# Longformer attention with a snake MLP on one core: where the lying keys and queries, w_out and the global columns are handled

## The chip, the cores and the metric

The kernel runs on one core of one Trainium2 chip. The metric is the device time of one execution in microseconds (us). The engines are named as in the profile: PE is the matrix engine (PEld its weight loads), DVE the vector engine, ACT the scalar engine with the activation functions, POOL the GpSimd engine, SP the engine that does nothing but issue DMAs. Each engine takes its instructions in the order in which the program emits them, so an instruction that waits holds up all that is emitted behind it on the same engine. POOL issues the DMAs that convert float32 to bfloat16 ("software" queue), SP those that do not ("hardware" queue).

## The reference

Inputs are q, k, v of 8 images (batch B) x 8 heads (H) x 576 tokens (S) x 64, eight global token indices, and the weights of a two layer MLP (512 to 2048 to 512). Attention is banded with a half width of 32, with rows and columns of the global tokens open:

```python
mask = np.abs(pos[:, None] - pos[None, :]) <= window          # window = 32
mask = mask | is_global[:, None] | is_global[None, :]
attn = softmax(where(mask, scale * q @ k.T, -1e9)); attn_out = attn @ v
h = x @ w_in                    # x: attn_out as 4608 rows of 512
s = np.sin(alpha * h)
g = h + s * s / (alpha + 1e-09)
out = g @ w_out
```

## The kernel before

**Stages.** The kernel treats one image (b = 0 to 7) at a time. `attention(b)` computes scores, exponentials, products with the values and denominators for four head pairs (hp) and leaves the normalised result, features on partitions, in `xTs[b]` (4 chunks of 128 features x 576 tokens). `gemm1(b)` multiplies with w_in in 16 groups (nt) of 128 features: eight matmuls of 288 columns a group, then on ACT the sine (`sb`), on ACT or DVE its square (`s2`; `ON_ACT...` lists the groups whose square is ACT's), on DVE the sum that is written into `H2[:, nt, ...]`. The result banks rotate over three PSUM tiles: group 0 zn, 1 zr, 2 zd, 3 zn and so on, so group nt + 3 has to wait for DVE's `H2` of group nt. Even images lie in columns 0 to 575 of H2, odd ones in 576 to 1151, and the 64 rows of the global tokens of all images in the last 64 columns.

**gemm2 as filler.** The second product, `gemm2(b)`, is a generator. It covers the 1152 columns of an image pair in blocks of 128: four blocks for even b, five for odd b, each block sixteen matmuls of 128x512, then an ACT copy `osb` and a store. `fill(n)` takes n matmuls from it wherever the program has put a `fill`: in `attention` 1 (START), then `FIRST` and `SECOND` around the two halves of the scores of each head pair, then `NEAR` and `MIDST`; in `gemm1` `PER_GROUP[nt]` after the matmuls of each group (`GROUP_LAST` for the last image). What is left at the end is done after the last `gemm1`, ahead of `gemm2_globals()` (the 64 global rows, result in zd) and of `gemm2(7)`.

**Global tokens.** Their rows of q, k, v of all images are gathered into `gq`, `gk`, `gv`, which lie in rows of H2 that are not yet in use (nt 13, 14, 15). `turn_kq()` turns them in bank `zo[1]` at the start of group 4 of `gemm1(0)`; `cast_globals_v()` on POOL converts gv. At the very end the normalised global rows (`global_rows`, lines 1064 to 1071) are put into the last columns of `xTs[7]`, and `put_globals()` (POOL, eight copies of 128x16) moves the columns of image 7's global tokens over the ordinary ones in H2. Where they go is computed in `load_columns()`: seven tiny DVE instructions, then eight register loads on POOL, behind head pair 3 of attention(5).

**Image 1's keys and queries.** They are loaded "lying" (48 rows of 48 x 64 values for each of k, q and each head parity t; `load_lying`, four DMAs of 288 KB on POOL) into the second halves of the tiles KD and VD. Attention(0) still uses these, so `load_lying(0)` is emitted behind the last head pair and `load_lying(1)` behind the last products. Then follow on POOL `cast_v(1)`, `load_w_out()` (four DMAs), and on SP `load_v(1)`. In `gemm1(0)` PE turns them in three thirds (`turn_lying`, 64 transposes each, at nt = 7, 9, 11) into the banks `zo[0]` (queries) and `zo[1]` (keys); `place_lying` copies each third to `KX[1]` (one DVE copy, at nt = 8, 10, 12) and to `QX[1]` (two ACT copies, at nt = 9, 11, 13). A third can be turned only when the copies of the one before have read the banks.

Of the kernel before, what the change touches and what calls it, by code (L numbers as in the profile page):

```python
# [10 lines left out]
ALU = mybir.AluOpType  # L11
AF = mybir.ActivationFunctionType
DT = mybir.dt
# [236 lines left out]
def kernel(  # L250
# [183 lines left out]
    def load_w_out():  # L434
# [11 lines left out]
    HK = HH * NT12  # L446
    nat = {w: H2[0 : D + HK, 2 + 3 * w : 5 + 3 * w, :].rearrange("p n c -> p (n c)")[:, 0 : KT * D] for w in (0, 1)}
    gq, gk, gv = [
        H2[0 : NG * B, nt, 0 : 2 * H * D].bitcast(DT.float32).rearrange("p (h d) -> p h d", d=D)
        for nt in (13, 14, 15)  # L450
    ]

    banks = mctx.enter_context(tc.tile_pool(name="banks", bufs=1, space=PSUM))
    zn, zd = [banks.tile([P, 2, 512], DT.float32, name=name) for name in ("zn", "zd")]
# [127 lines left out]
    load_v0((1, 2))  # L582
    load_w_in((1,))
    load_v0((3,))
    load_w_in((2, 3))
    load_vg0()
    gather(q, gq)

# [115 lines left out]
    for e, c0 in ((0, 20), (1, 16)):  # L704
        own = M2[:, :, e].rearrange("p t (x c) -> p t x c", x=2)[:, :, :, c0 : c0 + 24]
        nc.vector.tensor_tensor(out=own, in0=own, in1=farv[:, :, e], op=ALU.max)

    lie = [t[:, NHP * NT12 * D :] for t in (kflat, vflat)]

    def load_lying(t):  # L710

        for w, src in ((1, k), (0, q)):
            nc.gpsimd.dma_start(
                out=lie[t][D * w : D * w + NHP * NT12],
                in_=src[1].rearrange("(hp t) (i r) d -> t hp i (r d)", t=2, r=KT)[t],
            )

    R16 = KT // 3
    lain = [z.bitcast(DT.bfloat16)[:, 0 : R16 * NHP * NT12] for z in (zo[0][:], zo[1][:])]
# [219 lines left out]
    def attention(b, beside):  # L939
# [117 lines left out]
        inverse(last)  # L1057
        nc.scalar.preload_act_table(AF.Sin)
        fill(MIDST)
        numerators(last)  # L1060
        beside(NHP)
        after.release()

    def global_rows(bs):

        nc.vector.reciprocal(out=GR[:, :, :, bs], in_=GD[:, :, :, bs])
        if bs.stop == B:
            nc.vector.tensor_tensor(
                out=xTs[B - 1][:, :, S:SG], in0=GN[:].rearrange("p h j b -> p h (j b)"),
                in1=GR[:].rearrange("p h j b -> p h (j b)"), op=ALU.mult,  # L1070
            )


    spare = [kflat, vflat]
# [62 lines left out]


    ON_ACT = (1, 3, 5, 7, 9, 11, 13)
    ON_ACT_FIRST = (1, 3, 5, 7, 8, 10, 12, 14)  # L1140
    ON_ACT_SECOND = (1, 3, 5, 7, 9, 10, 12, 13)

    def gemm1(b):


        while len(waiting) > 1:
            fill(1)
        xT = xTs[b]
        r0 = (b % 2) * S
        more = b == B - 1  # L1150
        W = SG if more else S
        hr = tc.alloc_tile_pool(name="hr", bufs=1, space=PSUM)
        hs = {}

        def chunks(nt, cs, parts=slice(0, 2)):
            if nt not in hs:
                hs[nt] = (zn, None, zd)[nt % 3] or hr.tile([P, 2, 512], DT.float32, name="zr")
            h = hs[nt]
            for c in cs:
                for h_part, lo, hi in halves(h, W)[parts]:  # L1160
                    nc.tensor.matmul(  # L1161
                        out=h_part, lhsT=w_in[:, c, nt * P : (nt + 1) * P], rhs=xT[:, c, lo:hi],
                        start=(c == 0), stop=(c == CT - 1), skip_group_check=True,
                    )

        on_act = (ON_ACT_FIRST, ON_ACT_SECOND, ON_ACT)[min(b, 2)]
        for nt in range(NT):
            if b == 1 and nt in (10, 12):
                for which, t, y in PLACES[nt - 6 : nt - 4]:
                    place(2, which, t, y, nc.vector.tensor_copy)  # L1170
            if b == 0 and 8 <= nt < 14:
                third, late = divmod(nt - 8, 2)
                place_lying(1 - late, third, nc.scalar.copy if late else nc.vector.tensor_copy)
            if b == 0 and nt == 4:
                turn_kq()
            if b == 0 and nt == 10:

                cast_globals_v()
                for part in range(3):
                    place_globals(1, part, nc.gpsimd.tensor_copy)  # L1180
                load_vg(1)
            if nt == 0:

                for n in range(2):
                    chunks(n, range(CT - 1), slice(0, 2 - more))
                for n in range(2 * more):
                    chunks(n, range(CT - 1), slice(1, 2))
            chunks(nt, range(CT - 1, CT) if nt < 2 else range(CT))
            h = columns(hs[nt], W)
            fill((GROUP_LAST if more else PER_GROUP)[nt])  # L1190
            if b == 0 and nt in (7, 9, 11):
                turn_lying((nt - 7) // 2)
            sb = spool.tile([P, SG], DT.bfloat16, name="sb")
            nc.scalar.activation(out=sb[:, 0:W], in_=h, func=AF.Sin, scale=alphaT[:, nt : nt + 1])  # L1194
            s2 = spool.tile([P, SG], DT.bfloat16, name="s2")
            if nt in on_act:
                nc.scalar.activation(out=s2[:, 0:W], in_=sb[:, 0:W], func=AF.Square)  # L1197
            else:
                nc.vector.tensor_tensor(out=s2[:, 0:W], in0=sb[:, 0:W], in1=sb[:, 0:W], op=ALU.mult)  # L1199
            nc.vector.scalar_tensor_tensor(  # L1200
                out=H2[:, nt, r0 : r0 + W], in0=s2[:, 0:W], scalar=recipT[:, nt : nt + 1], in1=h,
                op0=ALU.mult, op1=ALU.add,
            )
        hr.release()


    columns_of = []

    def load_columns():

        ci = normp.tile([1, 4, NG], DT.int32, name="ci")
        cf = normp.tile([1, 4, NG], DT.float32, name="cf")
        nc.vector.tensor_copy(out=ci[:, 0], in_=gi32[:, 0::2])
# [11 lines left out]
        nc.vector.tensor_scalar(out=gcol[:], in0=cf[:, 3], scalar1=float(S), scalar2=None, op0=ALU.add)  # L1225
        for j in range(NG):
            columns_of.append(nc.gpsimd.value_load(gcol[0:1, j : j + 1], min_val=S, max_val=2 * S - 1))

    def put_globals():


        for j, c in enumerate(columns_of):
            g = 2 * S + j * B + B - 1
            nc.gpsimd.tensor_copy(out=H2[:, :, bass.ds(c, 1)], in_=H2[:, :, g : g + 1])  # L1234

    def gemm2(b):
        lo, hi = (0, 4) if b % 2 == 0 else (4, 9)
        for blk in range(lo, hi):
            ops = zo[(blk + b // 2) % 2]
            osb = osbp.tile([P, DM], DT.float32, name="osb")  # L1240
            parts = 2 if (b, blk) == (B - 1, hi - 1) else 1
            for part in range(parts):
                cols = slice(part * DM // parts, (part + 1) * DM // parts)
                if part:
                    ops = zd[:, 1]
                for nt in range(NT):
                    nc.tensor.matmul(  # L1247
                        out=ops[:, cols], lhsT=H2[:, nt, blk * P : (blk + 1) * P], rhs=w_out[:, nt, cols],
                        start=(nt == 0), stop=(nt == NT - 1), skip_group_check=True,
                    )  # L1250
                    yield True
                nc.scalar.copy(out=osb[:, cols], in_=ops[:, cols])  # L1252
                store(b, blk, osb, cols)

    def store(b, blk, osb, cols):
        c = blk * P
# [26 lines left out]
        )  # L1283


    waiting = []

    def fill(n):
        while n and waiting:
# [3 lines left out]
                n -= 1  # L1293

    START = 1
    FIRST, SECOND = (10, 6, 4, 4), (4, 4, 4, 4)

    NEAR, MIDST = 3, 6
    PER_GROUP = (0, 0, 5) + 11 * (1,) + (0, 0)
    GROUP_LAST = (0, 0, 3) + 13 * (1,)  # L1300

    def places_at(b_att, at):
# [43 lines left out]
    for b in range(B):  # L1346
# [27 lines left out]
    for c in (2, 3):  # L1374
        square_w(c)
        fill(NT)
    judge()
    fill(2 * NT * NT)
    mctx.close()
# [36 lines left out]
```

## Time and profile before

| | us |
|---|---|
| median of 3 runs | 358.66 (358.3 to 359.12) |
| the profiled execution, its own time | 358.42 |
| its span, first to last instruction | 356.7 |
| attention(0) and all loading ahead of it | 0 to 32.7 |
| gemm1(0) | 32.7 to 58.8 |
| attention(1), gemm1(1) | 58.8 to 76.3, 76.3 to 97.0 |
| attention(2), gemm1(2) | 97.0 to 114.0, 114.0 to 134.2 |
| attention(7), gemm1(7) | 284.2 to 301.5, 301.5 to 323.4 |
| rest of gemm2(6), global rows, gemm2(7), checks | 323.4 to 352.2 |
| last store, end of program | 352.2 to 356.7 |

Images 3 to 6 take the same 37 us each as image 2. The profile describes one execution; its times are counted from the start of the span, and 1.7 us of the execution lie outside it. A row of the timeline gives start, duration, engine, source line, operation, output and inputs with the number of instructions merged into it, and in brackets how long the engine was idle just before and what ended the wait. "issue" is a wait for nothing that the profile shows. Matmuls are pipelined: a single 128x512 matmul is shown with some 380 ns, while a row of them advances faster.

### The profile page before, as it was taken

How to read it: one execution, taken by the hardware profiler on the slowest of the kernel's cores; microseconds unless marked ns; L12 is line 12 of the kernel's file. 1: busy time of each engine (PE TensorE's matmuls, PEld its weight loads, DVE VectorE, ACT ScalarE, POOL GpSimd, SP SyncE). 2: the span in 40 equal slices, each digit the busy share in tenths (PEclk: the TensorE clock that was granted, in tenths of full speed). 3: DMA queues.
4: the chain of work that ended last, by engine and by line, in shares of the span. 5: the costliest groups of instructions: out<-in, count | busy, mean ns of one | idle time of the engine just before them, and what ended most of it. 6: DMA issues, size and time to landing. Idle time of an engine off the chain costs nothing.

```text
span 356.7 us, 10900 instructions
## 1 busy us (share of the span) xinstructions
PE 317.8 (89%) x4427; PEld 206.8 (58%) x4484; DVE 274.0 (77%) x536; ACT 286.3 (80%) x428; POOL 58.8 (16%) x85
## 2 busy tenths in 40 slices
PE   1579768999899999999999999899999998999994
PEld 1467555567555764576556655566566645565543
DVE  6785867788979787978798789878887877689630
ACT  6789768997888888988998889688988887878511
POOL 7965420050004000400040004000000000003300
PEclk9999999999999999999999999999999999999998
DMA  7999999669988926694859843993242011001232
GB/s 113 111 139 154 158 217 243 159 110 209 189 161 159 168 65 157 132 190 95 133 87 200 155 107 74 204 162 78 63 96 60 2 57 39 31 0 35 71 92 64
DMA packets 87762, 42.25 MB, mean 118 GB/s; under 512 B 72378, under 2 KB 82362, under 8 KB 87322
## 3 DMA queue, kind: packets, MB, share of 16 engines
q0 software_dynamic: 44944, 18.52, 43.6%
q1 hardware_dynamic: 42762, 22.98, 28.7%
q8 instruction: 36, 0.59, 0.7%
q14 instruction: 20, 0.16, 0.2%
HBM read 41.97 MB, written 20.77 MB: 176 GB/s over the span
## 4 chain that ended last, share of the span: by engine, by line
PE 54%; ACT 16%; DVE 13%; DMA 8%; issue 6%; POOL 0%; DVEq 0%; ACTq 0%; POOLq 0%
PE zo L1247 24%; PE zn L1161 8%; DVE H L1200 6%; PE zr L1161 5%; PE zd L1161 5%; ACT sb L1194 5%; PE ring L971 4%; DMA VD<-in_q_dram 3%; PE zd L1009 2%; DVE s L1199 2%; ACT L947 2%; ACT E L980 2%; PE zn L1009 2%; DMA VD<-vd 2%; ACT s L1197 2%
## 5 line engine op out<-in xcount | busy, mean ns | idle before, releaser
L1247 PE MATMUL zo<-w_out,H 128*128 128x512 bf16 (+1 forms) x519 | 135.2, 376 | 5.7 <-issue 4.8
L1161 PEld LDWEIGHTS <-w_in 128*128 128x128 bf16 x1024 | 99.1, 98 | 47.7 <-issue 15.3
L1247 PEld LDWEIGHTS <-H 128*128 128x128 bf16 x592 | 52.5, 98 | 44.9 <-DVE E L981 0.3
L1161 PE MATMUL zn<-xT,w_in 128*128 128x288 bf16 (+1 forms) x384 | 57.0, 287 | 6.8 <-DVE H L1200 3.4
L1194 ACT ACTIVATE sb<-zn,alphaT 128x576 bf16<-128x576 f32 (+1 forms) x48 | 35.7, 743 | 18.5 <-PE zn L1161 18.3
L1161 PE MATMUL zr<-xT,w_in 128*128 128x288 bf16 x320 | 47.7, 287 | 1.9 <-DVE H L1200 1.8
L980 ACT ACTIVATE E<-ring 128x720 bf16<-128x720 f32 x56 | 43.4, 776 | 7.4 <-PE ring L971 6.6
L1200 DVE SCALAR_TENSOR_TENSOR H<-s,recipT,zn 128x576 bf16<-128x576 bf16 (+1 forms) x48 | 39.5, 822 | 11.3 <-ACT s L1197 7.9
L1161 PE MATMUL zd<-xT,w_in 128*128 128x288 bf16 x320 | 46.3, 288 | 0.4 <-DVE H L1200 0.3
L1197 ACT ACTIVATE s<-sb 128x576 bf16<-128x576 bf16 (+1 forms) x58 | 40.0, 689 | 1.8
L981 DVE TENSOR_TENSOR E<-E,MASKT 128x720 bf16<-128x720 bf16 x56 | 29.6, 529 | 14.4 <-ACT E L980 14.2
L1199 DVE TENSOR_TENSOR s<-sb 128x576 bf16<-128x576 bf16 (+1 forms) x70 | 32.0, 458 | 10.5 <-ACT sb L1194 10.5
L1200 DVE SCALAR_TENSOR_TENSOR H<-s,recipT,zr 128x576 bf16<-128x576 bf16 (+1 forms) x40 | 32.9, 822 | 8.0 <-ACT s L1197 6.4
L1200 DVE SCALAR_TENSOR_TENSOR H<-s,recipT,zd 128x576 bf16<-128x576 bf16 (+1 forms) x40 | 32.9, 822 | 6.3 <-ACT s L1197 3.8
L1194 ACT ACTIVATE sb<-zr,alphaT 128x576 bf16<-128x576 f32 (+1 forms) x40 | 29.6, 741 | 7.7 <-PE zr L1161 7.7
L1194 ACT ACTIVATE sb<-zd,alphaT 128x576 bf16<-128x576 f32 (+1 forms) x40 | 29.5, 738 | 4.5 <-PE zd L1161 4.5
L1252 ACT COPY osb<-zo 128x512 f32<-128x512 f32 (+1 forms) x36 | 20.7, 575 | 13.0 <-PE zo L1247 6.7
L820 ACT ACTIVATE R<-L,shift 128x576 f32<-128x576 f32 x32 | 24.9, 778 | 0.5
L347 POOL COPY seen<-xT 1x1 bf16<-1x1 bf16 x4 | 1.7, 428 | 126.3 <-DVE GN L797 126.3
L1234 POOL COPY H<-H 128x16 bf16 x8 | 5.0, 630 | 103.8 <-DVE H L1200 103.4
L971 PEld LDWEIGHTS <-KX 64*64 64x64 bf16 x448 | 8.1, 106 | 14.3 <-issue 13.9
L1027 DVE TENSOR_TENSOR xT<-zn,R 128x576 bf16<-128x576 f32 x21 | 15.8, 753 | 0.8 <-ACT R L820 0.6
(185 smaller groups left out, 380.4 us busy)
## 6 DMA issues: line engine op xcount, KB each, us to landing
vd<-in_v_dram POOLq DMA_DIRECT2D x7, 576.0 KB, 13.9
kd<-in_k_dram POOLq DMA_DIRECT2D x6, 576.0 KB, 8.5
qd<-in_q_dram POOLq DMA_DIRECT2D x6, 576.0 KB, 10.4
VX<-vd SPq DMA_DIRECT2D x16, 168.0 KB
w_in<-in_moe_w_in_dram POOLq DMA_DIRECT2D x4, 512.0 KB, 6.1
w_out<-in_moe_w_out_dram POOLq DMA_DIRECT2D x4, 512.0 KB, 19.7
VD<-vd SPq DMA_DIRECT2D x12, 168.0 KB
out_dram<-osb SPq DMA_DIRECT2D x7, 256.0 KB
```

The source lines that it names most:

```text
L820: nc.scalar.activation(out=R[:], in_=L[:], func=AF.Exp, scale=-1.0, bias=shift[:, 0:1])
L971: nc.tensor.matmul(out=zs[half * D : (half + 1) * D, t, 0 : G3 * WCOL].rearrange("p (m x c) -> p m x c", x=2, c=60)[:, m % G3, :, c0:c1], ...
L980: nc.scalar.activation(out=Eg, in_=zs[:, :, 0 : G3 * WCOL], func=AF.Exp, scale=scale)
L981: nc.vector.tensor_tensor(out=Eg, in0=Eg, in1=MASKT[:, None, G3 * g : G3 * (g + 1), :].rearrange("p o m c -> p o (m c)").to_broadcast([P, ...
L1027: nc.vector.tensor_tensor(out=xT[:, hp, 0:S].rearrange("p (k m c) -> p k m c", k=4, c=KT), in0=tokens(nd(hp, 0)), in1=Rs[hp][:], op=ALU.mult,)
L1161: nc.tensor.matmul(out=h_part, lhsT=w_in[:, c, nt * P : (nt + 1) * P], rhs=xT[:, c, lo:hi], start=(c == 0), stop=(c == CT - 1), skip_group ...
L1194: nc.scalar.activation(out=sb[:, 0:W], in_=h, func=AF.Sin, scale=alphaT[:, nt : nt + 1])
L1197: nc.scalar.activation(out=s2[:, 0:W], in_=sb[:, 0:W], func=AF.Square)
L1199: nc.vector.tensor_tensor(out=s2[:, 0:W], in0=sb[:, 0:W], in1=sb[:, 0:W], op=ALU.mult)
L1200: nc.vector.scalar_tensor_tensor(out=H2[:, nt, r0 : r0 + W], in0=s2[:, 0:W], scalar=recipT[:, nt : nt + 1], in1=h, op0=ALU.mult, op1=ALU.add,)
L1247: nc.tensor.matmul(out=ops[:, cols], lhsT=H2[:, nt, blk * P : (blk + 1) * P], rhs=w_out[:, nt, cols], start=(nt == 0), stop=(nt == NT - 1) ...
L1252: nc.scalar.copy(out=osb[:, cols], in_=ops[:, cols])
```

## The change

Four things are changed, all in the order and place of work; what is computed stays the same.

1. `lie` moves into rows of H2 (nt 8 to 10 and 11 to 13). Both `load_lying` are now issued on POOL ahead of w_in's last two quarters, and behind these come `cast_v(1)` and `load_w_out()`, all ahead of attention(0). gq, gk and gv move to nt 14 and 15. In `gemm1(0)` the thirds are turned at nt = 2, 6, 9, and placed, keys and queries together, at nt = 3, 7, 10; `cast_globals_v`, `place_globals`, `load_vg(1)` come at nt 5 in place of 10, and `load_v(1)` behind them. The squares on ACT change from groups 8, 10, 12, 14 to 9, 11, 13, 14.
2. The seven DVE instructions of `load_columns` become `find_columns`, behind head pair 2 of attention(0); the register loads stay.
3. More of gemm2 is put into `fill`: FIRST[0] is 12 in place of 10, `PER_GROUP` gets one more matmul at nt = 14, and two more (`AFTER_COPY`) come two groups behind each group in which an `osb` copy was emitted.
4. `global_rows` is split: the reciprocal and the product of head pairs 0 to 2 are emitted ahead of the last numerators of attention(7), the product of pair 3 behind them. `put_globals` is split in groups 0 to 10, at nt = 11 of `gemm1(7)`, and 11 to 15, at the end. `gemm2(7)` begins with groups 0 to 10 of its first two blocks; 16 more of its matmuls come ahead of `judge()`.

```diff
     gq, gk, gv = [
-        H2[0 : NG * B, nt, 0 : 2 * H * D].bitcast(DT.float32).rearrange("p (h d) -> p h d", d=D)
-        for nt in (13, 14, 15)
+        H2[r : r + NG * B, nt, 0 : 2 * H * D].bitcast(DT.float32).rearrange("p (h d) -> p h d", d=D)
+        for r, nt in ((0, 14), (0, 15), (D, 14))
     ]
+    lie = [H2[:, n : n + 3, :].rearrange("p n c -> p (n c)")[:, 0 : KT * D] for n in (8, 11)]
     load_v0((3,))
+    load_lying(0)
+    load_lying(1)
     load_w_in((2, 3))
+    cast_v(1)
+    load_w_out()
     load_vg0()
...
-    lie = [t[:, NHP * NT12 * D :] for t in (kflat, vflat)]
...
         fill(MIDST)
+        if b == B - 1:
+            global_rows(slice(b, B))
+            global_columns(slice(0, last))
         numerators(last)
+        if b == B - 1:
+            global_columns(slice(last, NHP))
...
+    def global_columns(hps):
+        nc.vector.tensor_tensor(
+            out=xTs[B - 1][:, hps, S:SG], in0=GN[:, hps].rearrange("p h j b -> p h (j b)"),
+            in1=GR[:, hps].rearrange("p h j b -> p h (j b)"), op=ALU.mult,
+        )
...
-    ON_ACT_FIRST = (1, 3, 5, 7, 8, 10, 12, 14)
+    ON_ACT_FIRST = (1, 3, 5, 7, 9, 11, 13, 14)
...
         for nt in range(NT):
+            at_group[0] = (b, nt)
...
-            if b == 0 and 8 <= nt < 14:
-                third, late = divmod(nt - 8, 2)
-                place_lying(1 - late, third, nc.scalar.copy if late else nc.vector.tensor_copy)
+            if b == 0 and nt in (3, 7, 10):
+                for w, copy in ((1, nc.vector.tensor_copy), (0, nc.scalar.copy)):
+                    place_lying(w, (3, 7, 10).index(nt), copy)
             if b == 0 and nt == 4:
                 turn_kq()
-            if b == 0 and nt == 10:
+            if b == 0 and nt == 5:
                 cast_globals_v()
                 for part in range(3):
                     place_globals(1, part, nc.gpsimd.tensor_copy)
                 load_vg(1)
+                load_v(1)
+            if more and nt == SOON:
+                put_globals(slice(0, SOON))
...
             fill((GROUP_LAST if more else PER_GROUP)[nt])
-            if b == 0 and nt in (7, 9, 11):
-                turn_lying((nt - 7) // 2)
+            if nt and copied[0] == (b, nt - 2):
+                fill(AFTER_COPY)
+            if b == 0 and nt in (2, 6, 9):
+                turn_lying((2, 6, 9).index(nt))
...
+    SOON = 11
+    def put_globals(nts):
         for j, c in enumerate(columns_of):
             g = 2 * S + j * B + B - 1
-            nc.gpsimd.tensor_copy(out=H2[:, :, bass.ds(c, 1)], in_=H2[:, :, g : g + 1])
+            nc.gpsimd.tensor_copy(out=H2[:, nts, bass.ds(c, 1)], in_=H2[:, nts, g : g + 1])
...
+        def keep(blk, ops, osb, cols):
+            nc.scalar.copy(out=osb[:, cols], in_=ops[:, cols])
+            copied[0] = at_group[0]
+            store(b, blk, osb, cols)
+        full = slice(0, DM)
+        if b == B - 1:
+            for blk in (lo, lo + 1):
+                yield from products(blk, bank(blk), range(SOON), full)
...
-    FIRST, SECOND = (10, 6, 4, 4), (4, 4, 4, 4)
+    FIRST, SECOND = (12, 6, 4, 4), (4, 4, 4, 4)
+    AFTER_COPY = 2
-    PER_GROUP = (0, 0, 5) + 11 * (1,) + (0, 0)
+    PER_GROUP = (0, 0, 5) + 12 * (1,) + (0,)
...
-                if at == NHP - 1:
-                    load_lying(0)
+                if at == 2:
+                    find_columns()
                 if at == NHP:
-                    load_lying(1)
-                    cast_v(1)
...
-                    load_w_out()
-                    load_v(1)
...
-        if b == B - 1:
-            global_rows(slice(b, B))
         gemm1(b)
...
-    put_globals()
+    put_globals(slice(SOON, NT))
...
     for c in (2, 3):
         square_w(c)
         fill(NT)
+    fill(NT)
     judge()
```

More of the change, by code (lines that the diff above doesn't have):

```diff
@@ L448, with load_lying @@
     gq, gk, gv = [
-        H2[0 : NG * B, nt, 0 : 2 * H * D].bitcast(DT.float32).rearrange("p (h d) -> p h d", d=D)
-        for nt in (13, 14, 15)
-    ]
+        H2[r : r + NG * B, nt, 0 : 2 * H * D].bitcast(DT.float32).rearrange("p (h d) -> p h d", d=D)
+        for r, nt in ((0, 14), (0, 15), (D, 14))
+    ]
+    lie = [H2[:, n : n + 3, :].rearrange("p n c -> p (n c)")[:, 0 : KT * D] for n in (8, 11)]
+    def load_lying(t):
+        for w, src in ((1, k), (0, q)):
+            nc.gpsimd.dma_start(
+                out=lie[t][D * w : D * w + NHP * NT12],
+                in_=src[1].rearrange("(hp t) (i r) d -> t hp i (r d)", t=2, r=KT)[t],
+            )
     banks = mctx.enter_context(tc.tile_pool(name="banks", bufs=1, space=PSUM))
@@ L706 @@
         nc.vector.tensor_tensor(out=own, in0=own, in1=farv[:, :, e], op=ALU.max)
-    lie = [t[:, NHP * NT12 * D :] for t in (kflat, vflat)]
[L710 to L716, printed above, removed]
     R16 = KT // 3
@@ L1066, in global_rows @@
         nc.vector.reciprocal(out=GR[:, :, :, bs], in_=GD[:, :, :, bs])
[L1067 to L1071, printed above, removed]
+    def global_columns(hps):
+        nc.vector.tensor_tensor(
+            out=xTs[B - 1][:, hps, S:SG], in0=GN[:, hps].rearrange("p h j b -> p h (j b)"),
+            in1=GR[:, hps].rearrange("p h j b -> p h (j b)"), op=ALU.mult,
+        )
     spare = [kflat, vflat]
@@ L1204, in gemm1, with find_columns @@
         hr.release()
+        at_group[0] = None
     columns_of = []
-    def load_columns():
+    def find_columns():
         ci = normp.tile([1, 4, NG], DT.int32, name="ci")
@@ L1225, in load_columns @@
         nc.vector.tensor_scalar(out=gcol[:], in0=cf[:, 3], scalar1=float(S), scalar2=None, op0=ALU.add)
+    def load_columns():
         for j in range(NG):
             columns_of.append(nc.gpsimd.value_load(gcol[0:1, j : j + 1], min_val=S, max_val=2 * S - 1))
-    def put_globals():
+    SOON = 11
+    def put_globals(nts):
         for j, c in enumerate(columns_of):
             g = 2 * S + j * B + B - 1
-            nc.gpsimd.tensor_copy(out=H2[:, :, bass.ds(c, 1)], in_=H2[:, :, g : g + 1])
+            nc.gpsimd.tensor_copy(out=H2[:, nts, bass.ds(c, 1)], in_=H2[:, nts, g : g + 1])
@@ L1236, in gemm2, with bank, products @@
     def gemm2(b):
         lo, hi = (0, 4) if b % 2 == 0 else (4, 9)
+        def bank(blk):
+            return zo[(blk + b // 2) % 2]
+        def products(blk, ops, nts, cols):
+            for nt in nts:
+                nc.tensor.matmul(
+                    out=ops[:, cols], lhsT=H2[:, nt, blk * P : (blk + 1) * P], rhs=w_out[:, nt, cols],
+                    start=(nt == 0), stop=(nt == NT - 1), skip_group_check=True,
+                )
+                yield True
+        def keep(blk, ops, osb, cols):
+            nc.scalar.copy(out=osb[:, cols], in_=ops[:, cols])
+            copied[0] = at_group[0]
+            store(b, blk, osb, cols)
@@ L1238, in gemm2 @@
+        full = slice(0, DM)
+        if b == B - 1:
+            for blk in (lo, lo + 1):
+                yield from products(blk, bank(blk), range(SOON), full)
         for blk in range(lo, hi):
-            ops = zo[(blk + b // 2) % 2]
             osb = osbp.tile([P, DM], DT.float32, name="osb")
[L1241 to L1253, printed above, removed]
+            if (b, blk) == (B - 1, hi - 1):
+                for part, ops in enumerate((bank(blk), zd[:, 1])):
+                    cols = slice(part * DM // 2, (part + 1) * DM // 2)
+                    yield from products(blk, ops, range(NT), cols)
+                    keep(blk, ops, osb, cols)
+            else:
+                begun = SOON if b == B - 1 and blk < lo + 2 else 0
+                yield from products(blk, bank(blk), range(begun, NT), full)
+                keep(blk, bank(blk), osb, full)
@@ L1283, in gemm2_globals @@
         )
-    waiting = []
+    waiting, copied, at_group = [], [None], [None]
     def fill(n):
```

## The prediction

> **What bounds the kernel now.** I read the engines' busy shares first, then the chain of work that ended last, then busy time by stage.
>
> ```profile
> PE 317.8 (89%) x4427; PEld 206.8 (58%) x4484; DVE 274.0 (77%) x536; ACT 286.3 (80%) x428; POOL 58.8 (16%) x85
> ```
> ```profile
> 32.70:58.80 26.10, 20.33 (x329) 14.98 (x328) 18.49 (x30) 19.93 (x32) 9.24 (x13) 1.00 1.27 187
> 114.00:134.20 20.20, 19.55 (x154) 14.06 (x145) 16.32 (x27) 17.06 (x26) 0.00 (x0) 1.00 0.91 133
> 323.40:331.50 8.10, 8.10 (x39) 3.53 (x36) 7.04 (x10) 5.35 (x5) 4.78 (x7) 1.00 0.24 67
> ```
>
> The columns are span and busy time of PE, PEld, DVE, ACT, POOL, then clock, DMA share, GB/s. An ordinary gemm1 (114.0 to 134.2) leaves PE 0.65 us idle in 20.20, at full clock. gemm1(0) is different: nothing is full, and 26.10 us pass. The chain says what a group and a gemm2 matmul cost PE:
>
> ```profile
> 156.39 0.21 PE zo L1247
> 156.60 0.98 PE zr L1161 x8
> ```
> ```profile
> 323.61 7.99 PE zo L1247 x37
> 331.59 1.87 PE zd L1272 x32
> ```
>
> A group takes 0.98 us, a gemm2 matmul 7.99 / 37 = 0.216. Where PE has no idle time, a matmul costs 0.216 wherever it stands. So what the change gains between 58.8 and 352 is **PE idle time closed minus PE idle time opened**, not matmuls taken from the tail.
>
> By pitch a gemm1 has 16 x (0.98 + 0.216) = 19.1 us of work and 1.1 idle in its 20.20, by busy time 0.65; if the pitch is right, six such stages hide 2.7 us more than the waits listed below.
>
> The Trainium skill ("Trainium Kernel Development and Optimization", Performance Expectations) says that matmul busy time is a bad measure of how near a kernel is to its roofline, because matmuls are pipelined. The trace agrees: 37 matmuls of some 380 ns each pass in 7.99 us. [...]
>
> **1. find_columns.** Its seven DVE instructions stand in attention(5) now:
>
> ```profile
> 222.89 0.15 DVE L1213 COPY ci<-girow 1x8 int32<-1x8 int32 x1
> ...
> 224.04 0.16 DVE L1225 TENSOR_SCALAR gcol<-cf 1x8 int32<-1x8 f32 x1
> ```
> ```profile
> PE zn L1161 <- DVE H L1200: 1.3, 3, 0.5
> PE zn L1161 <- DVE GN L797: 1.2, 1, 1.2
> PE zn L1161 <- DVE xT L1068: 1.0, 1, 1.0
> PE zr L1161 <- DVE H L1200: 0.7, 3, 0.3
> PE zd L1161 <- DVE H L1200: 0.3, 1, 0.3
> ```
>
> The second fence lists PE's waits from 114 to 324 (total, times, longest), less two that do not matter. 224.20 - 222.89 = 1.31 us of DVE delay the normalising there; the single wait of 1.2 for GN, at the start of gemm1(5), is the price. It goes: **-1.1**, bounds 0 and -1.2. In attention(0) the same 1.31 us come ahead of head pair 3's masking:
>
> ```profile
> 29.74 1.22 DVE L847 TENSOR_TENSOR E<-E,MASK 128x480 bf16<-128x480 bf16 x3
> ```
> ```profile
> 31.77 0.63 ACT L813 ACTIVATE L<-zr 128x576 f32<-128x576 f32 x1
> 32.43 0.78 ACT L820 ACTIVATE R<-L,shift 128x576 f32<-128x576 f32 x1
> 33.23 1.28 ACT L929 ACT_TABLE_LOAD   x1
> 34.62 0.74 ACT L1194 ACTIVATE sb<-zn,alphaT 128x576 bf16<-128x576 f32 x1
> ```
>
> Masking would end at 30.96 + 1.31 = 32.27, PE's last denominators some 0.35 later, so the logarithm begins at 32.62 and not 31.77; inverse, table load and first sine follow without a gap. **+0.85**, bounds 0 (if the scores were late anyway) and +1.3.
>
> **2. Lying keys and queries.**
>
> ```profile
> 23.87 1.56 POOL L430 DMA_DIRECT2D w_in<-in_moe_w_in_dram  x2
> 30.57 0.65 POOL L713 DMA_DIRECT2D KD<-in_k_dram  x1 [5.13 <-ACT E L846]
> ```
> ```profile
> VD<-in_q_dram POOLq DMA_DIRECT2D x1, 288.0 KB, 10.7
> ```
> ```profile
> w_in<-in_moe_w_in_dram POOLq DMA_DIRECT2D x4, 512.0 KB, 6.1
> w_out<-in_moe_w_out_dram POOLq DMA_DIRECT2D x4, 512.0 KB, 19.7
> ```
> ```profile
> 36.84 1.14 PE L1161 MATMUL zn<-xT,w_in 128*128 128x288 bf16 x8 [1.03 <-DVE H L1200]
> ```
> ```profile
> 38.02 0.81 DVE L1200 SCALAR_TENSOR_TENSOR H<-s,recipT,zd 128x576 bf16<-128x576 bf16 x1
> ```
> ```profile
> 45.72 0.95 DVE L737 COPY KX<-zo 128x768 bf16<-128x768 bf16 x1
> ```
> ```profile
> PE zo L729 <- ACT QX L743: 2.1, 2, 1.2
> ```
>
> Four issues of 0.65 us take the place of w_in's at 23.87; the last begins at 25.8 and lands 10.7 later, at 36.5. The first turning now comes behind group 2, where PE stood idle for 1.03 us before 36.84 (37.7 with step 1's shift): just in time, and the turning fits the gap. The later thirds no longer wait for ACT's copies, so the 2.1 us go at best. But `turn_kq` ahead of group 4 writes the bank of the keys just turned and must now wait for their DVE copy, which stands behind group 2's H (38.02 + 0.81) and takes 0.95: it begins at 39.8 instead of 37.9, and group 4's matmuls, group 4's sine on ACT and all behind them wait with it. Of these 2 us the idle time of groups 6 and 7 takes back some; DVE still does the same three copies, and eight squares stay on ACT. I take **-0.5**, bounds -2.1 (nothing lost at turn_kq) and +1.5 (lying lands 3 us late, half of it covered by that wait). What POOL's queue puts back is covered: w_in's last quarters come at the latest at 27.4 + 10.7 + 6.1 = 44, for group 8 at 45; cast_v(1) and w_out have the same bytes ahead of them as before; POOL's value cast and global columns, behind these issues, have until attention(1) at 58.8, as have SP's load_vg(1) and load_v(1).
>
> **3. Attention(1).** Two more matmuls in a stage where PE is full: +0.43; two fewer in groups 10 and 11 of gemm1(1), where DVE places image 2's keys and queries as well: nearly nothing back. **+0.3**, bounds 0 and +1.4, since the 13th matmul there now needs w_out's last quarter (19.7 us to land) about 0.8 us after it came before.
>
> **4. Two more behind the first scores,** six stages:
>
> ```profile
> 97.44 2.11 PE L1247 MATMUL zo<-w_out,H 128*128 128x512 bf16 x9 [0.16 <-issue]
> 99.70 0.35 PE L971 MATMUL ring<-QX,KD 64*64 64x120 bf16 x14
> ```
>
> PE ends at 99.55 and waits 0.15 for the exponential. The two (0.43 us) close this: about 0.12 x 6 = **-0.7**, bounds 0 and -0.9.
>
> **5. gemm1(2) to gemm1(7).** The waits for H above are 1.3 + 0.7 + 0.3 = 2.3 us in seven places, one of 0.4 at a place that gets no matmul. The added one at nt 14 and the pairs behind a copy stand where the others are: **-1.6**, bounds 0 and -4.3 (by pitch).
>
> **6. Global rows.** The wait of 1.0 for xT (L1068) ahead of gemm1(7) goes, as the products of pairs 0 to 2 are done while PE works: **-0.9**, bounds 0 and -1.0.
>
> **7. The tail.** Fill counts: attention gives 50 matmuls a stage (52 after), gemm1 16 (17 and 2 a copy). Of the 496 of images 0 to 6, 36 are left behind gemm1(7) now, 5 after. The 31 x 0.216 = 6.7 us leave the tail, and the same 6.7 are paid in steps 3 to 5. But they covered something:
>
> ```profile
> 324.02 0.88 DVE L1200 SCALAR_TENSOR_TENSOR H<-s,recipT,zd 128x640 bf16<-128x640 bf16 x1
> 324.82 0.48 DVE L1199 TENSOR_TENSOR s<-sb 128x640 bf16<-128x640 bf16 x1
> 325.41 0.88 DVE L1200 SCALAR_TENSOR_TENSOR H<-s,recipT,zn 128x640 bf16<-128x640 bf16 x1
> 326.21 1.49 DVE L1090 TENSOR_TENSOR SQ<-xT 128x2560 bf16<-128x2560 bf16 x1
> ```
> ```profile
> 338.13 2.55 DVE L1082 TENSOR_TENSOR KD<-KD,VD 128x2048 bf16<-128x2048 bf16 x2
> ```
> ```profile
> L1234 POOL COPY H<-H x8: 254/465/1453, 326.4 to 331.6; 128x16 bf16 x8
> ```
>
> After five matmuls (323.4 + 1.1 = 324.5) the global rows need zd, free at 324.9: +0.4. Their last two need group 15's H at 326.3, which their own 1.87 us cover. Then 22 matmuls of gemm2(7) (4.7 us, to 331.6) cover POOL's second copies, which are shorter than the old ones (to 331.8). The check's sums end on DVE some 3 us earlier than 340.7, while PE comes there 6 us earlier, 3.5 of which the added 16 matmuls cover: +0.4. **+0.8**, bounds 0 and +1.7.
>
> **Sum.** -1.1 + 0.85 - 0.5 + 0.3 - 0.7 - 1.6 - 0.9 + 0.8 = -2.85. The profiled execution took 358.42 (span 356.7 and 1.7 around it), so 355.6; the median of the runs lies 0.24 above it: **355.8 us**.
>
> **Rivals.**
> - *Only moved.* The gaps re-form one group on, and steps 4 and 5 give nothing: 358.1. For it: the waits on H come from the length of the path through ACT and DVE. Against: they lie in front of single groups, next to copies. 0.12.
> - *All fits.* turn_kq's wait is absorbed and the tail opens no gap: 1.6 + 0.8 better, 353.4. For it: ACT and DVE are idle 6 and 7 us in gemm1(0). 0.13.
> - *POOL holds DVE.* The eight early copies fall among the squares of groups 12, 14 and 15. POOL's first copy now took 1.453 against 0.254 for the shortest, while SQ ran from 326.21 for 1.49: the two do exclude each other. If POOL is first, each of three squares (0.48) waits up to 0.254: +0.75, 356.6. 0.07. The Trainium skill ("SBUF — State Buffer", Who interferes with whom) has this rule: a DVE instruction with two SBUF inputs and a GpSimd one that reads SBUF block each other for a whole instruction. The trace agrees for DVE first; POOL first is not shown.
> - *Lying comes too late: slower.* PE stands at group 2 until it lands, and all else with it. turn_kq's wait covers it to about 39.8; beyond, each us costs one, and the sum of -2.85 is eaten at 42.7. It landed at 33.0 + 10.7 = 43.7 before; if it shares the engines with w_in's quarters and the gathers such that it lands no earlier than 43.7, 359.7. Against: its issue is 7 us earlier. 0.08.
>
> **Chances.** My forecast has 0.60. "Only moved" falls mostly within 0.2% (0.7 us, about what a measurement of this kernel can tell from no change). Faster 0.83, same 0.09, slower 0.08. The range leaves out "lying too late", half of "only moved" and the far end of "all fits": 353.4 to 358.1.
>
> **What would show it.** The first sine of gemm1(0) at 35.5; turn_kq behind a DVE copy; PE's waits for H in gemm1(2) to (7) under 0.8 in sum; no wait for GN ahead of gemm1(5) nor for L1068's successor ahead of gemm1(7); five matmuls, then a short wait for zd, behind gemm1(7). A first turning after 40, or the same waits as before, would make it wrong.

## The result and the profile after

The changed kernel takes **353.39 us** (351.78 to 354.62), the kernel before beside it 358.48 (357.99 to 359.79): a ratio of 0.9849, 95% interval 0.9829 to 0.9869. The sign was right and the size was not: 5.1 us faster, where 2.85 were forecast. The profiled execution took 353.31, its span is 351.6.

First the busy times of the changed kernel, then a few stages (columns as above: stretch, length, busy time of PE, PEld, DVE, ACT, POOL, then clock, DMA share, GB/s).

```profile
PE 324.5 (92%) x4484; PEld 207.1 (59%) x4484; DVE 276.1 (79%) x537; ACT 287.1 (82%) x428; POOL 60.7 (17%) x93
```
```profile
115.70:135.90 20.20, 20.20 (x156) 14.33 (x148) 16.06 (x26) 17.08 (x26) 0.00 (x0) 1.00 1.04 155
...
324.80:347.00 22.20, 21.85 (x156) 12.19 (x153) 15.29 (x30) 11.62 (x14) 6.18 (x9) 1.00 0.26 68
35.10:59.90 24.80, 21.59 (x332) 15.69 (x331) 18.12 (x29) 19.39 (x31) 4.60 (x8) 0.92 1.41 211
```

An ordinary gemm1 (first row) is as long as before, 20.20 us, holds three matmuls more by the fill counts (the profile before lacks 57 matmul records, so its rows count too few), and PE's records leave no idle time in it. gemm1(0) (last row) is 1.3 us shorter although PE's granted clock fell to 0.92 there. The list of PE's waits from 115 to 324 us, seven rows before, is one row:

```profile
PE zn L1172 <- DVE H L1217: 0.4, 1, 0.4
```

The ends of the stages, read from the timelines, split the gain. The last column is a second profiled execution of the same program, `after_again` below.

| | before | after | after, again |
|---|---|---|---|
| first scores of attention(2) begin at | 96.93 | 98.61 | 97.34 |
| from there to the start of gemm1(7) | 203.84 | 204.74 | 204.73 |
| from there to PE's last matmul | 50.96 | 43.57 | 43.56 |
| both | 254.80 | 248.31 | 248.29 |

From attention(2) on the program repeats itself to 0.02 us and gains **6.5**; another 0.3 is gained behind PE's last matmul (4.99 to 4.69 us to the end of the span). Six of the kernels below, whose edits all act ahead of attention(2), take 248.28 to 248.67 in this part, so differences under 0.4 are not read here. The start loses something, and how much differs between executions of the same instructions: the changed kernel twice and two variants that differ only behind gemm1(6) (`rows_back`, `put_whole`) reach attention(2) at 98.61, 97.34, 97.15 and 96.80, on average 0.55 us later than before, of which there is one profile only. The medians put the loss higher: they gain 5.1 (358.48 to 353.39, and 357.49 to 352.38 when measured again), and 6.5 + 0.3 - 5.1 leaves some 1.7 lost ahead of attention(2), as in the first of the four, if the rest repeats as in the profiles. So what happens from attention(2) on can be read from single executions, and the start only where a difference is well over a microsecond or a row names its cause.

In the tail the order is the new one. The timeline of the changed kernel, PE and then POOL:

```profile
324.96 1.46 PE L1266 MATMUL zo<-w_out,H 128*128 128x512 bf16 x6
326.48 1.94 PE L1310 MATMUL zd<-w_out,H 128*64 128x256 bf16 x32
328.35 4.92 PE L1266 MATMUL zo<-w_out,H 128*128 128x512 bf16 x22
333.49 2.76 PE L1266 MATMUL zo<-w_out,H 128*128 128x512 bf16 x12 [0.22 <-POOL H L1256]
```
```profile
321.02 2.50 POOL L1256 COPY H<-H 128x11 bf16 x8 [95.41 <-DVE H L1217]
327.87 5.56 POOL L1256 COPY H<-H 128x5 bf16 x8 [4.36 <-DVE H L1217]
```

Six matmuls are left behind gemm1(7) where 37 were; the global rows follow without a wait, and the 22 matmuls of gemm2(7) that need only groups 0 to 10 stand beside POOL's second copies. The first of these (a row of the chain of waits) ends 0.07 us behind DVE's sum of two SBUF operands (a row of the timeline) that began ahead of it, and each of the next four ends 0.07 us behind one of DVE's next sums:

```profile
327.91 1.38 POOL H L1256
```
```profile
327.73 1.49 DVE L1101 TENSOR_TENSOR SQ<-xT 128x2560 bf16<-128x2560 bf16 x1
```

### The profile page after: what moved, and what is told of

It reads as the page before. It is cut to its first block, busy times and chain, and to the rows that moved or that the text cites. A ratio compares the mean times of both kernels' runs of the same rounds, so it can differ in the third digit from the quotient of the medians.

```text
span 351.6 us, 10962 instructions
## 1 busy us (share of the span) xinstructions
PE 324.5 (92%) x4484; PEld 207.1 (59%) x4484; DVE 276.1 (79%) x537; ACT 287.1 (82%) x428; POOL 60.7 (17%) x93
## 4 chain that ended last, share of the span: by engine, by line
PE 43%; issue 29%; DVE 5%; ACT 3%; POOL 2%; POOLq 1%; DVEq 0%; ACTq 0%
PE zo L1266 21%; PE zn L1172 6%; PE zr L1172 5%; PE zd L1172 4%; PE ring L975 3%; DVE H L1217 2%; POOL H L1256 2%; PE zd L1013 2%; PE zn L1013 1%; POOLq L1248 1%; ACT sb L1211 1%; DVE xT L1031 1%; ACT s L1214 1%; DVE KD L369 1%; PE zd L1266 1%
## 5 line engine op out<-in xcount | busy, mean ns | idle before, releaser
L1266 PE MATMUL zo<-w_out,H 128*128 128x512 bf16 (+1 forms) x576 | 149.4, 377 | 0.2 <-POOL H L1256 0.2
L1172 PE MATMUL zr<-xT,w_in 128*128 128x288 bf16 x320 | 48.7, 291 | 1.5 <-DVE H L1217 1.5
L824 ACT ACTIVATE R<-L,shift 128x576 f32<-128x576 f32 x32 | 24.8, 776 | 0.6
L1256 POOL COPY H<-H 128x11 bf16 (+1 forms) x16 | 7.2, 450 | 100.6 <-DVE H L1217 99.8
L343 POOL DMA_DIRECT2D vd<-in_v_dram x7 | 16.4, 2337 | 0.1
```

Source lines behind the costliest of these rows:

```text
L343: nc.gpsimd.dma_start(out=cast[b, "vd"][:], in_=v[b].rearrange("h s d -> s h d"))
L824: nc.scalar.activation(out=R[:], in_=L[:], func=AF.Exp, scale=-1.0, bias=shift[:, 0:1])
L1172: nc.tensor.matmul(out=h_part, lhsT=w_in[:, c, nt * P : (nt + 1) * P], rhs=xT[:, c, lo:hi], start=(c == 0), stop=(c == CT - 1), skip_group ...
L1266: nc.tensor.matmul(out=ops[:, cols], lhsT=H2[:, nt, blk * P : (blk + 1) * P], rhs=w_out[:, nt, cols], start=(nt == 0), stop=(nt == NT - 1) ...
```

## The experiments

Twelve runs follow: eleven edits of the changed kernel, and the changed kernel again. Ratios are to the kernel before in the same job; the changed kernel has 0.9849 (0.9829 to 0.9869), and 0.9873 (0.9843 to 0.9903) when run again.

**no_fill: the old fill counts.**

```diff
-    FIRST, SECOND = (12, 6, 4, 4), (4, 4, 4, 4)
-    AFTER_COPY = 2
+    FIRST, SECOND = (10, 6, 4, 4), (4, 4, 4, 4)
+    AFTER_COPY = 0
-    PER_GROUP = (0, 0, 5) + 12 * (1,) + (0,)
+    PER_GROUP = (0, 0, 5) + 11 * (1,) + (0, 0)
```

> The fill counts of before (10 behind the first scores, none behind a copy, eleven ones in gemm1's groups), all else as changed: 31 matmuls go back behind gemm1(7), 6.7 us. Theory A: at each of PE's waits the last matmul's record outlasts its pitch by 380 - 216 = 0.16 us, so the gaps were longer than the waits listed, and the moved matmuls cost only 0.4 x 6 in the attentions and 0.7 in gemm1(2) to (6): about 4 us slower than the changed kernel, 357.4. Theory B, the prediction's: the gaps are the waits as listed, 0.7 + 1.6 of them filled, less the 0.4 for zd in the tail: 1.9 us slower, 355.3.

0.9963 (0.9938 to 0.9988), 357.56 us; the difference of the ratios is 0.0114, 4.1 us (3.2 against the changed kernel run again). From attention(2) on PE takes 252.28, 4.0 more than the changed kernel. Theory A has the total, and its reading of the waits holds; its split does not quite, as shown below. PE's waits from 115 to 324 us in this run, and one of them in the timeline:

```profile
PE zn L1172 <- DVE H L1217: 1.1, 3, 0.5
PE zr L1172 <- DVE H L1217: 0.7, 3, 0.3
PE zd L1172 <- DVE H L1217: 0.3, 1, 0.3
```
```profile
132.77 1.14 PE L1172 MATMUL zd<-xT,w_in 128*128 128x288 bf16 x8
134.39 1.14 PE L1172 MATMUL zn<-xT,w_in 128*128 128x288 bf16 x8 [0.48 <-DVE H L1217]
```

The eight matmuls that begin at 132.77 need 0.98 us of PE and their row says 1.14, because the last one's record runs on for its own length. The bracket counts from the end of the record: 134.39 - 133.91 = 0.48. PE could have taken something else from 133.75: 0.64. There are seven such places, so the 2.1 us listed are 2.1 + 7 x 0.16 = 3.2. Counted over all matmuls of gemm1(2) to (7), what lies between two starts beyond the pitch is 5.3 us in this run and 1.9 in the changed kernel: 3.4 filled. The attentions fill another 1.1: with twelve matmuls more, 2.6 us by pitch, the six together grow by only 1.45 (101.51 to 102.96). The tail takes 0.5 back: with 31 matmuls less, 6.7 us, it is 6.2 shorter. 3.4 + 1.1 - 0.5 makes the 4.0.

**rows_back: the global rows at the head of gemm1(7).**

```diff
     fill(MIDST)
-        if b == B - 1:
-            global_rows(slice(b, B))
-            global_columns(slice(0, last))
     numerators(last)
-        if b == B - 1:
-            global_columns(slice(last, NHP))
...
+        if b == B - 1:
+            global_rows(slice(b, B))
+            global_columns(slice(0, NHP))
         gemm1(b)
```

> Reciprocal and product of the global rows go back to the head of gemm1(7), in one piece, all else as changed. The prediction's step: PE waits 1.0 us there for the product again, and about 0.9 comes back, 354.3. Rival: the wait comes back but the idle time of the groups behind it and the tail take it up: 353.4 to 353.6.

0.9877 (0.9854 to 0.99), 354.31 us. From attention(2) on 249.42, 1.1 more, all of it in gemm1(7); the tail behind is as long as before. The wait is back, with nothing to take it up:

```profile
PE zn L1169 <- DVE xT L1076: 1.0, 1, 1.0
```

**cols_5_3 and cols_5_1: find_columns back in attention(5).** The second has it two head pairs earlier (`at == 1`).

```diff
-                if at == 2:
-                    find_columns()
...
             if b_att == 5 and at == 3:
+                find_columns()
                 load_columns()
```

> find_columns goes back to attention(5), ahead of load_columns, and leaves attention(0); everything else is as changed (353.4 us). Theory A: in the changed trace its first copy of 1x8 integers took 1.91 us, against 0.15 in attention(5) before, while POOL was issuing DMAs (2.25 us for vd's, 1.30 for w_out's), and the wait of 2.6 us for the masked scores that follows also costs clock (0.95 in that stage): out of attention(0) it gives back some 2.4 us, and it costs about 1.2 in attention(5) again, so 352.2. Theory B, the prediction's: 1.31 us of DVE work in either place, 0.85 on the path in attention(0) and 1.1 in attention(5), so 353.6. The wait for the masked scores tells it apart in the profile: about 0.8 us by A, 1.7 or more by B.

> find_columns in attention(5) two head pairs earlier than load_columns, so neither in attention(0) nor next to the normalising. Theory A (POOL's issues hold the copy in attention(0)): some 2.4 us less than the changed kernel and little new in attention(5), 351.0 to 351.5. Theory B (1.31 us of DVE work wherever it stands): 0.85 us less, 352.5.

0.9889 (0.9865 to 0.9914), 354.9 us, and 0.9894 (0.9841 to 0.9947), 354.47: neither is faster than the changed kernel, against theory A and B alike. Yet the parts go as theory A has them. The wait for the masked scores in attention(0), 1.2 to 2.6 us in the four executions of the changed start, is gone, gemm1(0) begins at 33.03 and 32.27 (33.28 to 35.13 in the four), and attention(1) at 57.54 and 56.01 (58.36 to 59.91). In attention(5) the old wait returns:

```profile
PE zn L1172 <- DVE GN L801: 1.2, 1, 1.2
```

attention(5) takes 18.42 and 18.27 us, 17.21 in the changed kernel: 1.2 and 1.1, at either place. That explains a part. The rest is lost in attention(1) and gemm1(1), where both kernels have a wait that the changed one has not. The chain of waits of cols_5_1 there:

```profile
37.81 23.42 DMA w_out<-in_moe_w_out_dram
61.23 0.04 issue
61.27 0.38 PE zo L1266
```

PE had begun gemm2(0) and stood 2.4 us (0.4 in cols_5_3) for the 13th matmul, the first to need w_out's last quarter. Both stand another 0.8 at the first numerators of attention(1), and cols_5_3 1.1 for a sum in gemm1(1). A theory W came from this: that quarter lands at 61 us, whatever PE does. In the fourteen profiles it lands between 59.57 and 62.15.

**cols_g1 and w_out_two: find_columns out of the way, then w_out asked for later.** cols_g1 has the first two hunks, w_out_two all.

```diff
+            if b == 0 and nt == 12:
+                find_columns()
             if b == 0 and nt == 4:
                 turn_kq()
...
-                if at == 2:
-                    find_columns()
...
-        if b == B - 1:
+        soon = {0: 12, B - 1: SOON}.get(b, 0)
+        if soon:
             for blk in (lo, lo + 1):
-                yield from products(blk, bank(blk), range(SOON), full)
+                yield from products(blk, bank(blk), range(soon), full)
...
-                begun = SOON if b == B - 1 and blk < lo + 2 else 0
+                begun = soon if blk < lo + 2 else 0
```

> find_columns stands at the head of group 12 of gemm1(0), where DVE has idle time and POOL issues no DMA; all else as changed (353.4 us). Its first copy should take 0.15 us there, gemm1(0) start at about 32.3 and attention(1) at about 56.5, as without it in attention(0), and attention(5) keep its 17.2 us. Theory W (w_out's last quarter lands at 61 whatever PE does, as in the two kernels with find_columns in attention(5)): PE waits 2 us or more for w_out behind the first scores, gemm1(1) starts no earlier than 76.0, and the time is 352.4. Theory N (the wait for w_out there was an accident of those runs): gemm1(1) starts at 73.8 and the time is 350.0.

> The same, and gemm2(0) begins with the first 12 matmuls of its first two blocks, so that w_out's last quarter is asked for 12 matmuls later in attention(1). Theory W: the wait for it goes, since 12 matmuls and the scores and products of one to two head pairs between them take over 2.5 us, and gemm1(1) starts about 2 us earlier than with find_columns moved alone: 350.4. If the bound there is something else (DVE and ACT of attention(1), the turning of image 2), the gain is under 0.5.

0.9861 (0.9825 to 0.9897), 353.36 us, and 0.9856 (0.983 to 0.9881), 352.86. At group 12 the first copy takes 0.15 us, and gemm1(0) begins at 31.96 and 32.91. In cols_g1 the wait stands where theory W put it:

```profile
51.94 0.15 DVE L1233 COPY ci<-girow 1x8 int32<-1x8 int32 x1
```
```profile
56.16 2.55 PE L1268 MATMUL zo<-w_out,H 128*128 128x512 bf16 x11
60.96 0.38 PE L1268 MATMUL zo<-w_out,H 128*128 128x512 bf16 x1 [2.25 <-DMA w_out<-in_moe_w_out_dram]
```

gemm1(1) begins at 75.34, between the two forecasts. With two blocks begun the wait for w_out is gone, but gemm1(1) begins only 0.2 us earlier, at 75.17, and attention(2) no earlier: 96.86 against 96.47. PE now stands 1.1 us at the first numerators of attention(1), at a wait whose end the trace does not name. So W is right about w_out and wrong in that a gain lies behind it.

**lie_back: keys and queries lie in KD and VD again,** loaded, turned and placed as before, with cast_v(1), w_out and load_v(1) behind attention(0), the cast of the global values at group 10 and the squares on ACT of the kernel before.

```diff
-    load_lying(0)
-    load_lying(1)
     load_w_in((2, 3))
-    cast_v(1)
-    load_w_out()
...
-            if b == 0 and nt in (2, 6, 9):
-                turn_lying((2, 6, 9).index(nt))
+            if b == 0 and nt in (7, 9, 11):
+                turn_lying((nt - 7) // 2)
```

> Image 1's keys and queries lie in the second halves of KD and VD again, are loaded behind attention(0)'s head pair 3, and are turned behind groups 7, 9 and 11; cast_v(1), w_out and load_v(1) are issued where they were. All else is as changed, find_columns in attention(0) too. The prediction's step 2 says that this part is worth 0.5 us: 353.9. Theory A: POOL issues no DMA from 25.4 to 30.5 then, so find_columns' first copy takes 0.15 us and not 1 to 2, gemm1(0) starts at 33.5; and the part is worth about 2 us between gemm1(0)'s start and attention(1), which then starts at 60.0 and more: 353.5 to 355 in sum, the two effects against each other. The copy's duration and the length of gemm1(0) (26.1 us before, 24.8 after) tell more than the time.

0.99 (0.9874 to 0.9926), 354.48 us: 1.8 us slower than the changed kernel by the ratios, whose intervals nearly touch, and 1.0 slower than the same kernel run again, where they overlap. The two effects are both there. gemm1(0) takes 27.1 us from its first matmul to the first scores of attention(1) (26.2 in the kernel before), against 24.8 to 25.1 in the four executions of the changed start: 1.1 to 2.3 us for this part. (lie_back and the four each have 3.41 us at half the clock in this stage, the kernel before has none; see the last section. With that alike, the part is worth 2.0 to 2.3.) And find_columns' first copy is short where POOL issues nothing. DVE in this run, in the changed kernel, and the changed kernel's POOL:

```profile
29.84 0.15 DVE L1228 COPY ci<-girow 1x8 int32<-1x8 int32 x1
```
```profile
29.24 1.91 DVE L1231 COPY ci<-girow 1x8 int32<-1x8 int32 x1
```
```profile
28.72 2.25 POOL L343 DMA_DIRECT2D vd<-in_v_dram  x1
30.43 1.30 POOL L436 DMA_DIRECT2D w_out<-in_moe_w_out_dram  x1
```

The copy ends 0.18 us behind POOL's issue for `vd` (28.72 + 2.25 = 30.97, 29.24 + 1.91 = 31.15). Six executions have the copy inside that issue, begun between 0.5 and 1.8 us into it; it takes 1.91, 1.10, 0.94, 1.93, 1.85 and 0.63 us, and in each it ends 0.17 or 0.18 us after the issue. The next issue, w_out's, begins before that and does not hold the copy.

**kq_later, cols_kq, all_three: turn_kq a group later, alone and with the two edits above.**

```diff
-            if b == 0 and nt == 4:
+            if b == 0 and nt == 5:
                 turn_kq()
-            if b == 0 and nt == 5:
+            if b == 0 and nt == 6:
                 cast_globals_v()
```

> turn_kq moves from group 4 to group 5 of gemm1(0), and the cast of the global values, place_globals, load_vg and load_v from group 5 to 6; all else as changed. PE waited 1.8 us at turn_kq for the keys' copy on DVE, and ACT 3.4 for group 4. If this stall is what gemm1(0) loses, the stage gets 1.0 to 1.8 us shorter, and 0.7 to 1.3 of it is left until w_out's landing stops it: 352.3. If the idle time of the groups behind takes it back anyway, or VD's later loads cost the same, 353.4.

> find_columns at group 12 of gemm1(0) and turn_kq at group 5, both alone tried already. If the two are independent, attention(1) starts at 54.5 (55.9 with the first alone, 1.4 to 2.2 us less with the second); by theory W w_out's last quarter then holds PE for over 3 us behind the first scores, gemm1(1) starts at 75.3 as with the first alone, and the time is 352.5 to 353. If nothing holds it, 351.

> Both, and gemm2(0) begun with 12 matmuls of two blocks. By theory W the 12 matmuls lie in front of the wait, so gemm1(1) starts 1 to 2 us earlier than with the two alone: 351. If the first 60 us are bound by the DMA engines as a whole (their share is 0.9 and more in nearly every slice up to 60 us), another transfer takes w_out's place and the time stays at 352.5.

0.9843 (0.981 to 0.9876), 0.9875 (0.9844 to 0.9905) and 0.984 (0.9801 to 0.9879); 352.21, 353.25 and 352.76 us, beside 352.38 for the changed kernel in the job of the last two. PE's wait at turn_kq in the changed kernel and in kq_later:

```profile
42.49 1.09 PE L773 MATMUL zo<-idf,H 64*128 64x64 f32 x8 [1.78 <-DVE KX L741]
```
```profile
PE zo L773 <- DVE KX L741: 0.8, 1, 0.8
```

The stage is 2 us shorter (22.8) and attention(2) begins at 97.50, inside the spread of the changed kernel. How much of the 2 us is turn_kq's is not shown: the four executions have 3.41 us at half the clock within this stage, kq_later only the last of such a stretch at its start. Where the clock stays at 1.00 throughout the stage, cols_kq and all_three take 24.2 and 22.9 for the 23.9 of both cols_g1 and w_out_two.

cols_kq's attention(1) begins at 57.17 and not at the expected 54.5. Its PE waits 1.2 us at the first turning, for the keys that are still being loaded, as it does in cols_5_1:

```profile
36.80 0.21 PE L733 MATMUL zo<-identb,H 48*64 48x48 bf16 x2 [1.30 <-DMA H<-in_k_dram]
```

Later cols_kq waits 1.8 for w_out; all_three, with no wait for it, stands here:

```profile
65.75 0.78 PE L1013 MATMUL zn<-E,VX 56*64 56x88 bf16 x26 [2.03 <-issue]
```

These are the numerators' operands E and VX, and which of their producers was late is not shown. In all, seven rearrangements of the start put attention(2) between 96.47 and 98.62, the unaltered start between 96.80 and 98.61. What PE, DVE or ACT win ahead of 56 us is mostly taken again by waits that end between 60.8 and 67.8 us, w_out's landing where the trace names one. **None is shown to beat the changed kernel.**

**after_again and put_whole.** The first is the changed kernel; the second copies the global columns in one step behind gemm1(7).

```diff
-            if more and nt == SOON:
-                put_globals(slice(0, SOON))
...
-    put_globals(slice(SOON, NT))
+    put_globals(slice(0, NT))
```

> The changed kernel unaltered, beside the two that follow: 353.4, and find_columns' first copy between 0.9 and 1.9 us in attention(0), as in the four executions that had it beside POOL's issues.

> The global columns are copied in one step of all 16 rows behind gemm1(7) again, all else as changed. gemm2(7)'s first 22 matmuls, which stand at 328.4 to 333.3 in the changed kernel, need the copies and wait until 331.8: about 3.4 us slower, 356.8. If the eight early copies cost gemm1(7) their 2.5 us (the rival in which POOL holds DVE), that is got back and it is 355.6 or less, with gemm1(7) 0.75 us or more shorter.

after_again: 352.38 us, copy 1.85. put_whole: 1.0053 (1.0024 to 1.0082), 359.47 us, **slower than the kernel before.** The timelines of PE and POOL show why:

```profile
324.64 1.94 PE L1308 MATMUL zd<-w_out,H 128*64 128x256 bf16 x32
331.77 10.43 PE L1264 MATMUL zo<-w_out,H 128*128 128x512 bf16 x41 [5.19 <-POOL H L1254]
```
```profile
326.04 5.67 POOL L1254 COPY H<-H 128x16 bf16 x8 [102.23 <-DVE H L1215]
```

The expected 3.4 us took the copies' end from the kernel before, whose gemm1(7) ended earlier in the span; the wait is 5.2, and PE takes 254.56 us from attention(2) on, 6.3 more. The rest of the loss is the clock: behind the wait it is halved, as this row shows (clock 0.50), and the first seven matmuls stand 0.39 to 0.43 us apart where 0.216 is usual, 1.4 us in all.

```profile
331.30:334.60 3.30, 2.83 (x7) 1.04 (x8) 3.18 (x8) 1.09 (x1) 1.34 (x3) 0.50 0.16 34
```

gemm1(7) is 21.47 us long from its first matmul to the start of its last, 21.46 in the changed kernel: the eight early copies cost it nothing.

## Why the prediction fell short

Point by point, from attention(2) on first, where one execution decides. The steps there summed to -3.5, and -6.5 came:

- **Step 1, attention(5): right.** Forecast -1.1; undone, it costs 1.2 and 1.1 in that stage. (Image 5 took 38.4 us before, not the 37 of the images beside it.)
- **Step 4: too small.** Forecast -0.7, bounds 0 and -0.9; 1.1 by no_fill. The wait of 0.15 at these places, too, was counted from the end of the last matmul's record (see step 5).
- **Step 5: the one that failed, by its size.** It summed the listed waits, "-1.6, bounds 0 and -4.3 (by pitch)"; 3.4 were there, so this step is 1.8 of the 3.0 us that were missing. A wait is listed from the end of the last matmul's record, which runs 0.16 us beyond PE's work, and each of seven waits hides that much. The pitch bound was in the text and was the one to take. It was still too wide: of the 5.3 us beyond the pitch that no_fill shows in these stages, 1.9 stay in the changed kernel too. The Trainium skill ("Trainium Kernel Development and Optimization", Performance Expectations) says that matmul busy time is a bad measure of how close a kernel is to its roofline, because matmuls are pipelined. no_fill agrees with it, 3.4 us filled against 2.1 listed.
- **Step 6: right.** Forecast -0.9, measured 1.1 in rows_back.
- **Step 7: 0.4 too dear.** From gemm1(7)'s last matmuls to PE's end 6.3 us went (28.43 to 22.11), with the 6.7 removed and 0.4 of new waits, forecast 0.8. There is no wait for zd, since a sixth matmul is left and covers it, and the only wait seen is 0.22 for POOL. One premise was wrong: POOL's second copies are not shorter. Eight copies of 5 rows took 5.56 us, as long as eight of 16 (5.46), because the first five end just behind DVE's sums (rows above). The 22 matmuls cover them all the same.

Undone one at a time, find_columns (1.2), the global rows (1.1) and the fill counts (4.0) make 6.3 of the 6.5.

The start was forecast at 0.85 - 0.5 + 0.3 = +0.65. The four profiles have -0.13 to +1.68, on average +0.55, by **two errors that work against each other**: gemm1(0) begins 0.6 to 2.4 us later than before (1.3 on average, forecast 0.85), and from there to attention(2) 0.6 to 0.9 is won back (forecast 0.2). That the average comes near is luck. By the medians the start loses some 1.7; what makes them higher stays open. The prediction has no term for the clock, which was 1.00 in the stages that it read and is halved for one or two stretches of this start (last section).

- **Step 1, attention(0): too cheap.** 0.85 was worked out from seven instructions of 1.31 us in all. They took 3.2 in the first profile (2.0 in the shortest of the four), since the first stood until POOL's issue for vd was done, and gemm1(0) began 2.4 us later than before in that execution; its first sine came at 37.36, where the prediction had 35.5. The step treated find_columns alone; it was step 2 that moved POOL's issues beside it. By the Trainium skill ("SBUF — State Buffer", Who interferes with whom) a copy on DVE in a two-port mode and GpSimd, which needs the same ports for writing descriptors (an inference of the Trainium skill), exclude each other for a whole instruction. The durations above agree, with POOL first; which mode this copy of eight integers ran in, no run here shows.
- **Step 2: too small.** Not 0.5 but 1.1 to 2.3 us in gemm1(0). The wait at turn_kq came as described (1.78, forecast as 1.9), and the stage still gained 1.1 against the kernel before. Whether the later groups took some of the wait back is open, as kq_later's 2.0 us are mixed with the clock.
- **Step 3** is within the spread; the late quarter of w_out named there as its upper bound is what holds the faster variants.

Of the rivals, *only moved* is refuted by no_fill, *POOL holds DVE* in gemm1(7) by put_whole, *lying too late* by the first turning, in the changed kernel's timeline at 38.48 with no wait of its own; the margin is small, since five of the six kernels whose gemm1(0) begins earlier, between 31.96 and 33.03, wait 0.2 to 1.5 us for this load there. *All fits*, at 353.4, named the right total for other reasons: it expected the gain at turn_kq and in the tail.

```profile
38.48 0.70 PE L733 MATMUL zo<-identb,H 48*64 48x48 bf16 x64
39.58 1.14 PE L1172 MATMUL zn<-xT,w_in 128*128 128x288 bf16 x8 [0.40 <-DVE H L1217]
```

## What to carry to other kernels

Size idle time on the matrix engine by the starts of its matmuls and their pitch: at each listed wait the last record covers time in which another matmul would have fitted. A part that moves DMA issues on GpSimd changes what the vector engine's small copies cost beside them, so price two edits that meet in one stage together. Beside the rest of the change, splitting the late copies decided between a gain and a loss: work taken out of the tail is a gain only if something else still covers what it covered.

## What was not expected of the hardware

A DVE copy of eight integers took 0.15 us alone and 0.63 to 1.93 us beside the issue of one GpSimd DMA (2.25 us), ending 0.17 or 0.18 us after it each time.

PE's granted clock fell in the changed kernel's start. The stretches of the changed kernel and of cols_g1:

```profile
10.00:35.00 25.00, 16.35 (x216) 14.19 (x217) 20.61 (x57) 19.66 (x44) 19.07 (x27) 0.95 1.16 134
35.00:60.00 25.00, 21.78 (x342) 15.89 (x343) 18.22 (x29) 19.59 (x31) 4.60 (x8) 0.92 1.41 211
```
```profile
10.00:35.00 25.00, 18.89 (x242) 15.85 (x242) 18.81 (x53) 21.14 (x43) 19.74 (x28) 1.00 1.15 137
35.00:60.00 25.00, 19.82 (x331) 13.88 (x331) 20.29 (x37) 19.72 (x31) 4.24 (x8) 1.00 1.41 211
```

Within them the clock (third figure from the end) is halved in two stretches of 3.41 us, of which these two rows of the changed kernel show the inside:

```profile
32.40:35.70 3.30, 2.85 (x31) 2.67 (x32) 2.42 (x9) 1.43 (x3) 0.75 (x1) 0.50 1.10 194
42.70:46.00 3.30, 3.30 (x19) 2.30 (x19) 1.22 (x3) 0.34 (x1) 0.00 (x0) 0.50 1.79 184
```

The waits ahead of it in the changed kernel are 2.6 us at the masked scores and 1.78 at turn_kq; cols_g1 has none of the first and 1.2 at the second. Behind turn_kq eight gemm1 matmuls took 2.10 us in the changed kernel, where 1.14 is usual:

```profile
43.52 2.10 PE L1172 MATMUL zr<-xT,w_in 128*128 128x288 bf16 x8
```

In the fourteen profiles the clock is halved in this way thirteen times between 30 us and the end of the work, each time for 3.41 us. In the 3.41 us ahead of each, PE was idle by its records for 1.4 to 3.4 us in sum; one such stretch with 1.6 us, in rows_back, was not followed by a drop. It is not a matter of these profiles alone: the mean granted clock was 0.987 to 0.992 in eleven of the changed kernel's twelve executions, and 0.995 to 1.000 in the 33 of the kernel before for which it is on record. What a drop costs in the start, and what decides whether the clock drops, was not tried by itself.
